# Order of three transfers, of weight splits and of gathers in a kernel of clustered attention and two-level experts

## The chip, the cores and the metric

The kernel runs on one core of one Trainium2 chip. The metric is the device time of one execution in microseconds; a kernel is executed several times and its median is taken. The kernel before takes 748.74 us (median of 3 runs, 743.39 to 748.81).

## The reference

What is computed is an attention over clusters, whose output is the input of a mixture of experts with two levels of routing. Cut to what matters (shapes: batch 4, 8 heads, 768 positions, head size 64, 16 clusters; then 3072 tokens of 512, 4 groups of 4 experts, hidden size 1024):

```python
q_assign = argmax(einsum('bhsd,hcd->bhsc', q_n, c_n), axis=-1)     # normalised q, centroids
k_assign = argmax(einsum('bhsd,hcd->bhsc', k_n, c_n), axis=-1)
mask = q_assign[:, :, :, None] == k_assign[:, :, None, :]
scores = where(mask, scale * matmul(q, k.transpose(0, 1, 3, 2)), -1e9)
scores = scores - max(scores, axis=-1, keepdims=True)
attn = exp(scores) / (sum(exp(scores)) + 1e-9)
x = matmul(attn, v)  ->  rows of [3072, 512]

g_idx = argmax(x @ w_group);  g_w = softmax(x @ w_group)[g_idx]
for g in groups:                      # tokens of group g
    e_idx = argmax(xg @ w_expert[g]); e_w = softmax(...)[e_idx]
    for e in experts of g:            # tokens of expert e
        h = maximum(xg[mask_e] @ w1[g, e], 0.0)
        out[tok_idx] = (g_w * e_w)[:, None] * (h @ w2[g, e])
```

## The kernel before, in words

The work is one stream of matmuls on TensorE with the other engines beside it. Float32 operands are split in two float16 halves (a high part, and what is left of it), and a product is made of three products of halves.

**Attention.** Heads go through in turn (32 of them, numbered over batch and head). A coarse pass (`coarse`) makes scores and their maxima; `rowmax` (from L326) transposes the maxima, ScalarE copies them from PSUM to the tile `mr` (L345), and a transfer on SyncE's queue (SP) puts them into row 80 of the head's operand tile A (L347). The fine pass (`fine`, L355 on) makes the scores with two matmuls (L360 with A, L361 with B), exponentials on ScalarE (L365), the low part on GpSimd or VectorE (L372), and `av` multiplies by V (L392). The head needs its `mr` before the first L360 of its fine pass.

**Routing.** When a batch's heads are done, `Router.decide` finds group and expert of each token, and GpSimd scatters token number and gate into a table in HBM, one slot per token, by expert (L711).

**Expert A.** `Experts.first` takes the expert with the most tokens so far and loads and splits its weights while attention still runs. `fetch` (L889 on) is a generator that the attention's schedule advances a step at a time ("yield"): it waits until the third of the four batches has been routed, waits READ = 5 further steps, reads the expert's slots from the table (`tabA`, three transfers, L893) and the table itself (`tb`, L894) on SP's queue, converts the ids, gathers the rows on GpSimd (L975) into the tiles `qx`, `kx`, `vx`, with 3 steps behind each, and transposes them by three SP transfers into `xTA` (L919). Part A is the feed-forward network of that expert on these rows (matmuls of L1013, up, and L1035, down), with 288 slots.

**Ranks.** `ranks` (L1314) goes through the remaining work: rank -1 takes the last batch's tokens of expert A (128 slots, `xTB`), ranks 0 to 14 take one expert each, sorted by their number of tokens, with 288 slots and fewer. A rank has 8 steps, each one of the up matmuls (12 matmuls into a PSUM tile `psh`, evacuated by ScalarE to `hh` at L1015 and split by VectorE to `hl` at L1016), a piece of the down matmuls of the rank before (L1035 into `psy`, evacuated at L1038 `yh` and L1039 `yl`, or L1049), `settle` (L1075, L1088), the transposition of the next rank's tokens (`tokens`, L985 and L987, at step 5), and the making of weights: `stream` is a generator which loads 512 KB of float32 weights per step (`load_chunk`, L801, on SP's queue into tile `st`, five loads ahead, six tiles) and splits them (`split_chunk`: high part on ScalarE L808 or GpSimd L810, low part on VectorE L811). There are 8 parts a rank, four of w1 and four of w2; FILL says at which steps of a rank the generator is advanced. The tiles of one rank's w1 are wh0a and wl0a, of the next rank's wh0b and wl0b, those of w2 wh1b or wh. A tile of `psh` is free again when `hl` has been made; there are three.

**Order.** Each engine executes its instructions in the order in which the program lists them. The scheduler places instructions by the dependencies and by `issue_after(x)`, which puts what follows behind instruction x in the list of x's engine. SP's and GpSimd's queues of transfers are lists in the same way: a transfer that waits holds what stands behind it.

## Time and profile before

| | us |
|---|---|
| median of 3 runs | 748.74 (743.39 to 748.81) |
| the profiled execution, its time | 746.08 |
| its span (first to last instruction) | 744.3 |
| around the span | 1.8 |
| mean granted clock of TensorE | 0.989 of full speed |

Times in the trace are counted from the start of the span. Busy time is that in which an engine executes an instruction; the rows of a timeline give the start, the duration, the instruction with what it writes and reads and, in brackets, how long its engine had been idle and what ended that. "SPq" is the queue of transfers that SyncE issues. The span has 26030 instructions.

### The profile page before, as it was taken

To read this page: it belongs to the slowest core of one execution; us is meant where nothing else is said; L and a number is where in the kernel's file an instruction comes from. 1 tells how busy PE (TensorE), PEld (TensorE's weight loads), DVE (VectorE), ACT (ScalarE), POOL (GpSimd) and SP (SyncE) were. 2 spreads that over 40 slices of the span, in tenths; PEclk is the share of its full clock that TensorE was granted. 3 is DMA by queue.
4 is the path that set the end of the run, shared out by engine and by line. 5 is a ranking of instruction groups with operands and counts; after the bars stand their busy time and mean duration, and the time that the engine had idled before them with its cause. 6 is when DMAs were issued, how large, how long until landed. Compare 5 with 4: busy or idle time off the path is not lost.

```text
span 744.3 us, 26030 instructions
## 1 busy us (share of the span) xinstructions
PE 712.3 (96%) x10672; PEld 608.8 (82%) x10672; DVE 601.0 (81%) x1246; ACT 473.2 (64%) x913; POOL 498.4 (67%) x526
## 2 busy tenths in 40 slices
PE   5899999999999999999899989999999999999996
PEld 3677888887788888888687866887789999999995
DVE  5999989898998989988977547766778888898861
ACT  4558798897979879777873364444444455555542
POOL 9678897899988999889962354244554545564522
PEclk9999999999999999999999989999999999999999
DMA  8856737457584756517650886877688688888811
GB/s 256 192 163 174 199 90 192 124 152 156 102 207 98 174 137 132 120 21 185 130 106 26 219 303 202 258 220 219 214 259 258 221 275 279 246 281 277 262 62 51
DMA packets 115719, 134.74 MB, mean 181 GB/s; under 512 B 34963, under 2 KB 85651, under 8 KB 115592
## 3 DMA queue, kind: packets, MB, share of 16 engines
q1 hardware_dynamic: 109820, 119.61, 58.7%
q0 software_dynamic: 5616, 13.35, 5.1%
q8 instruction: 85, 1.39, 0.8%
q14 instruction: 42, 0.34, 0.2%
q10 hardware_dynamic: 156, 0.03, 0.0%
HBM read 93.20 MB, written 14.11 MB: 144 GB/s over the span
## 4 chain that ended last, share of the span: by engine, by line
PE 63%; DVE 18%; ACT 6%; issue 5%; DMA 3%; POOL 2%; another core or an unknown queue 1%; POOLq 0%; SPq 0%; ACTq 0%; DVEq 0%
PE psh L1013 15%; PE pso L392 11%; PE psy L1035 10%; PE psf L360 6%; PE psf L361 5%; PE psc L318 5%; DVE mpart L321 5%; PE psy L1049 3%; ACT p L365 2%; DMA st<-w 2%; PE psm L251 2%; DVE wl0a L811 1%; PE psm L985 1%; PE psm L1075 1%
## 5 line engine op out<-in xcount | busy, mean ns | idle before, releaser
L372 POOL TENSOR_TENSOR pl<-p 128x512 f16<-128x512 f32 x212 | 218.2, 1052 | 28.1 <-ACT p L365 25.7
L365 ACT ACTIVATE p<-psf 128x512 f32<-128x512 f32 x288 | 171.4, 598 | 51.4 <-PE psf L361 41.7
L321 DVE TENSOR_REDUCE mpart<-psc 128x1 f32<-128x512 f32 (+1 forms) x282 | 189.0, 682 | 17.6 <-PE psc L318 15.6
L392 PE MATMUL pso<-V,pl 128*128 128x65 f16 x2040 | 165.0, 193 | 0.0
L360 PE MATMUL psf<-A 82*128 82x384 f16 (+2 forms) x576 | 144.2, 275 | 2.5 <-DMA A<-mr 2.0
L361 PE MATMUL psf<-B 128*128 128x384 f16 (+2 forms) x576 | 144.1, 275 | 0.0
L392 PEld LDWEIGHTS <-p 128*128 128x128 bf16 x1776 | 124.4, 98 | 23.3 <-issue 1.2
L392 PEld LDWEIGHTS <-pl 128*128 128x128 f16 x2040 | 134.7, 97 | 1.3 <-issue 0.4
L392 PE MATMUL pso<-V,p 128*128 128x65 f16 x1776 | 132.9, 193 | 0.0
L318 PE MATMUL psc<-A 80*128 80x512 f16 (+1 forms) x376 | 107.0, 328 | 4.5 <-DVE mpart L321 3.2
L1016 DVE SCALAR_TENSOR_TENSOR hl<-psh,hh 128x160 f16<-128x160 f32 (+14 forms) x136 | 50.3, 370 | 66.0 <-ACT hh L1015 50.2
L372 POOL TENSOR_TENSOR pl<-p,ph 128x512 f16<-128x512 f32 x66 | 76.0, 1158 | 21.0 <-POOL pl L372 8.8
L1015 ACT ACTIVATE hh<-psh 128x160 f16<-128x160 f32 (+14 forms) x136 | 46.3, 345 | 66.7 <-PE psh L1013 62.4
L1013 PE MATMUL psh<-xT,wh0a 128*128 128x288 f16 (+7 forms) x512 | 74.7, 255 | 0.0
L1013 PE MATMUL psh<-xT,wh0b 128*128 128x272 f16 (+6 forms) x448 | 65.2, 254 | 1.7 <-DVE xT L987 0.7
L975 POOL DMA_INDIRECT xg<-xbuf,ri x32 | 40.0, 1251 | 38.7 <-PE psm L985 21.8
L361 PEld LDWEIGHTS <-B 128*128 128x128 f16 x576 | 56.8, 99 | 10.7 <-issue 1.9
L360 PEld LDWEIGHTS <-A 82*128 82x128 f16 x576 | 55.7, 98 | 11.5 <-DMA A<-mr 2.0
L1013 PE MATMUL psh<-xT,wl0a 128*128 128x288 f16 (+7 forms) x256 | 64.0, 255 | 0.0
L1089 POOL DMA_INDIRECT out_dram<-y,ri x32 | 38.4, 1200 | 32.3 <-ACT y L1088 25.9
L1013 PE MATMUL psh<-xT,wl0b 128*128 128x272 f16 (+6 forms) x224 | 55.9, 253 | 0.0
L1013 PEld LDWEIGHTS <-wh0a 128*128 128x128 f16 x512 | 46.6, 98 | 4.9
(327 smaller groups left out, 1657.9 us busy)
## 6 DMA issues: line engine op xcount, KB each, us to landing
st<-w SPq DMA_DIRECT2D x128, 512.0 KB
B<-parts SPq DMA_DIRECT2D x64, 192.0 KB
kx<-kT SPq DMA_DIRECT2D x16, 384.0 KB
qx<-qT SPq DMA_DIRECT2D x16, 384.0 KB
vx<-vr SPq DMA_DIRECT2D x16, 384.0 KB
A<-parts SPq DMA_DIRECT2D x32, 192.0 KB
xbuf<-xs SPq DMA_DIRECT2D x16, 384.0 KB
A<-mk SPq DMA_DIRECT2D x56, 24.0 KB
```

The source lines that it names most:

```text
L318: last["mm"] = nc.tensor.matmul(out=pc[:, off:off + k1 - k0], lhsT=QA[h % 8][0:80, c * P:(c + 1) * P], rhs=KA[h % 8][0:80, k0:k1], start=T ...
L321: nc.vector.tensor_reduce(out=(mp[:, 0, 0:1], mp[:, :, 1], mp[:, 1, 0:1])[i], in_=pc.rearrange("p (a x) -> p a x", a=n), axis=AX.X, op=ALU ...
L360: nc.tensor.matmul(out=o, lhsT=KA[h % 8][0:82, ks], rhs=QA[h % 8][0:82, q0:q1], start=True, stop=False)
L361: nc.tensor.matmul(out=o, lhsT=KBs[h][:, ks], rhs=QBs[h][:, q0:q1], start=False, stop=True)
L365: cfg["exp"] = nc.scalar.activation(out=p32, in_=pf, func=AF.Exp, scale=QK / (SQ * SQ))
L372: lo = (nc.vector if u in (EARLY if h < 2 else DVE_LO[h % 8] if h < NH - 2 else DVE_END) else nc.gpsimd).tensor_tensor(out=pl, in0=p32, in ...
L392: nc.tensor.matmul(out=O[:, col:col + v.shape[-1]], lhsT=p[:, bs], rhs=v, start=c == 0 and q == 0 and i == 0, stop=c == NCH - 1 and i == l ...
L975: self.got = nc.gpsimd.indirect_dma_start(out=xg[0:n].rearrange("p k a x -> p (k a x)"), out_offset=None, in_offset=bass.IndirectOffsetOnA ...
L1013: self.mm = nc.tensor.matmul(out=ph[:, 0:M], lhsT=w[:, k, fs], rhs=xT[:, a, k], start=i == 0, stop=i == 3 * KD - 1)
L1015: nc.scalar.activation(out=hh[:, f], in_=ph[:, 0:M], func=AF.Relu)
L1016: self.ev = nc.vector.scalar_tensor_tensor(out=hl[:, f], in0=ph[:, 0:M], scalar=0.0, in1=hh[:, f], op0=ALU.max, op1=ALU.subtract)
L1035: self.mm = nc.tensor.matmul(out=py[:, 0:M], lhsT=w[:, f, d * P:(d + 1) * P], rhs=a[:, f], start=i == 0, stop=i == len(prods) - 1)
```

## The change

Three things are altered. First, `rowmax` keeps its transfer in cfg["mr"], and `fetch` waits two more steps before it reads the table, and lists these reads behind the latest such transfer; the steps behind each gather become two instead of three. Second, FILL: in rank -1 the generator of weights is advanced at steps 0, 2, 4 and 6 alone (four parts instead of eight), in rank 1 twice in each of the first four steps (twelve instead of eight), in all other ranks once in each step as before. Third, the gathers of rank k + 2 are written down at rank k instead of those of rank k + 1.

```diff
@@ -344,7 +344,7 @@
         mr = sm.tile([NCH, P], F16, name="mr")
         nc.scalar.copy(out=mr, in_=tp[0:NCH, 0:P])
         ready.add(("max", h))
-        last["mr"] = (nc.scalar if h == 2 else nc.sync).dma_start(out=QA[h % 8][80:81].rearrange("o (c x) -> o c x", x=P), in_=mr)
+        last["mr"] = cfg["mr"] = (nc.scalar if h == 2 else nc.sync).dma_start(out=QA[h % 8][80:81].rearrange("o (c x) -> o c x", x=P), in_=mr)
 
     def fsegs(u):
 
@@ -743,7 +743,7 @@
     ADD = 5
     SLOTS = 13
     SLT = 12
-    FILL, SETTLE, TOK = (0, 1, 2, 3, 4, 5, 6, 7), 2, 5
+    FILL, SETTLE, TOK = {-1: (1, 0, 1, 0, 1, 0, 1, 0), 1: (2, 2, 2, 2, 1, 1, 1, 1)}, 2, 5
     HI = (0, 1, 0, 1, 0, 1, 0, 1)
     LEAD = 12
 
@@ -886,9 +886,9 @@
         self.tb = self.small("tb", [R.E, self.nt * P, 2])
         while R.done < R.B - 2:
             yield
-        for _ in range(READ):
+        for _ in range(READ + 2):
             yield
-        with self.after():
+        with self.after(), self.tc.issue_after(self.cfg["mr"].ins) if "mr" in self.cfg else ExitStack():
             for t, n in enumerate(sz):
                 R.reads(nc.sync.dma_start(out=tab[0:n, t], in_=tv[t * P:t * P + n]))
             R.reads(nc.sync.dma_start(out=self.tb, in_=R.table.rearrange("(e s) w -> e s w", s=R.BS)[0:R.E, 0:self.nt * P]))
@@ -911,7 +911,7 @@
             if rows:
                 with self.tc.issue_after(self.cfg["lo"].ins) if "lo" in self.cfg else ExitStack():
                     self.gather(ids[0:n, t:t + 1], n, xgs[t], rows)
-            for _ in range(3):
+            for _ in range(2):
                 yield
         xTA = self.wa.tile([P, KD, 2, CA], F16, name="xTA")
         self.xTA = xTA.rearrange("p k a m -> p a k m")
@@ -1314,11 +1314,12 @@
     def ranks(self, bg):
 
         E, sizes = self.R.E, self.sizes
-        xT, xgs, down = self.xTB, self.xg0, iter(())
+        xT, nxt, down = self.xTB, self.xg0, iter(())
         for k in range(-1, E - 1):
             M = self.caps[k] if k >= 0 else P
-            if 0 <= k < E - 2:
-                xgs = self.gathers(k + 1)
+            xgs = nxt
+            if k < E - 3:
+                nxt = self.gathers(k + 2)
             h = []
             up = self.up(xT, M, self.weights_of(k, 0) if k >= 0 else self.WA[0:2], h)
             for i in range(8):
@@ -1328,7 +1329,7 @@
                 next(down, None)
                 if i == (self.SETTLE if k >= 0 else 6):
                     self.settle()
-                if i in self.FILL:
+                for _ in range(self.FILL[k][i] if k in self.FILL else 1):
                     with ExitStack() as order:
                         for op in (self.kept, self.turned, self.got, self.yev[min(1 + i // 2, 3)]) if k < 0 else (self.ev,):
                             order.enter_context(self.tc.issue_after(op.ins))
```

What the edits move in the engines' lists is seen at three places.

SyncE's queue, near the end of attention. `A_171<-mr` and `A_172<-mr` are the row maxima of two heads, `tabA` and `tb` the reads of the table, `xTA` the three transposes that part A reads, `xTr` a transpose for the routing, `xbuf` the store of token rows; ISA rows stand in front of transfers whose address comes from a register. Before:

```order
L893 ISA
L893 DMA tabA<-table 128x2
L347 DMA A_171<-mr 1x6x128
L893 ISA
L893 DMA tabA<-table 128x2
L893 ISA
L893 DMA tabA<-table 32x2
L894 DMA tb<-table 16x768
L347 DMA A_172<-mr 1x6x128
L919 DMA_TRANSPOSE xTA<-qx 128x8x128
L598 DMA xbuf<-xs 128x6x256
L919 DMA_TRANSPOSE xTA<-kx 128x8x128
```

After:

```order
L347 DMA A_171<-mr 1x6x128
L893 ISA
L893 DMA tabA<-table 128x2
L893 ISA
L893 DMA tabA<-table 128x2
L893 ISA
L893 DMA tabA<-table 32x2
L894 DMA tb<-table 16x768
L347 DMA A_172<-mr 1x6x128
L598 DMA xbuf<-xs 128x6x256
L919 DMA_TRANSPOSE xTA<-qx 128x8x128
L613 DMA_TRANSPOSE xTr<-xs 128x12x128
```

The first row maxima now stand in front of the three reads of the table, the second where they stood; the transposes from `qx` and `kx` each stand one place later, behind the store and the transpose of `xTr`; in both lists the one from `vx` is the last of the three.

ScalarE's list, rank -1. `yh` is the evacuation of part A's result, `wh0a`, `wh0b` and `wh1b` are high parts of weights, each of which waits for its own load; the loads in order have the semaphores DMAHW4, 5, 6, 7, 0, 1, 2, 3. Before:

```order
L1205 CAST xT<-psm 128x512 [waits PE_49]
L808 ACTIVATE wh0a<-st 128x2x512 [waits DMAHW4_49]
L808 ACTIVATE wh0a<-st 128x2x512 [waits DMAHW5_49]
L1038 ACTIVATE yh<-psy 128x288 [waits PE_49]
L808 ACTIVATE wh0a<-st 128x2x512 [waits DMAHW6_49]
L808 ACTIVATE wh0a<-st 128x2x512 [waits DMAHW7_49]
L1038 ACTIVATE yh<-psy 128x288 [waits PE_49]
L808 ACTIVATE wh0b<-st 128x2x512 [waits DMAHW0_49]
L1015 ACTIVATE hh<-psh 128x128 [waits DVE_49,PE_49]
L808 ACTIVATE wh0b<-st 128x2x512 [waits DMAHW1_49]
L1015 ACTIVATE hh<-psh 128x128 [waits PE_49] x2
L808 ACTIVATE wh1b<-st 128x4x256 [waits DMAHW2_49]
```

After:

```order
L1205 CAST xT<-psm 128x512 [waits PE_49]
L808 ACTIVATE wh0a<-st 128x2x512 [waits DMAHW4_49]
L808 ACTIVATE wh0b<-st 128x2x512 [waits DMAHW0_49]
L1038 ACTIVATE yh<-psy 128x288 [waits PE_49]
L808 ACTIVATE wh0a<-st 128x2x512 [waits DMAHW5_49]
L808 ACTIVATE wh0b<-st 128x2x512 [waits DMAHW1_49]
L808 ACTIVATE wh1b<-st 128x4x256 [waits DMAHW2_49]
L1038 ACTIVATE yh<-psy 128x288 [waits PE_49]
L1015 ACTIVATE hh<-psh 128x128 [waits DVE_49,PE_49]
L808 ACTIVATE wh0a<-st 128x2x512 [waits DMAHW6_49]
L1015 ACTIVATE hh<-psh 128x128 [waits PE_49]
L808 ACTIVATE wh0a<-st 128x2x512 [waits DMAHW7_49]
```

In front of the first `yh` here stands the split of the fifth load (DMAHW0) in place of the second's; three splits instead of two precede the second `yh`.

VectorE's list, same place. `ri` holds the ids for the gathers of ranks 0 on, `rg` the gates, `yl` the low part of part A's result, `hl` the low part of the hidden values. Before:

```order
L1211 TENSOR_SCALAR bi<-psm 128x1
L1212 TENSOR_SCALAR bg<-psm 128x1
L811 SCALAR_TENSOR_TENSOR wl0a<-st,wh0a 128x2x512 x2
L1103 CAST ri<-psm 128x48
L1104 TENSOR_SCALAR rg<-psm 128x48
L1039 SCALAR_TENSOR_TENSOR yl<-psy,yh 128x288
L811 SCALAR_TENSOR_TENSOR wl0a<-st,wh0a 128x2x512 x2
L1039 SCALAR_TENSOR_TENSOR yl<-psy,yh 128x288
L811 SCALAR_TENSOR_TENSOR wl0b<-st,wh0b 128x2x512
L1016 SCALAR_TENSOR_TENSOR hl<-psh,hh 128x128 x3
```

After:

```order
L1211 TENSOR_SCALAR bi<-psm 128x1
L1212 TENSOR_SCALAR bg<-psm 128x1
L811 SCALAR_TENSOR_TENSOR wl0a<-st,wh0a 128x2x512
L1039 SCALAR_TENSOR_TENSOR yl<-psy,yh 128x288
L1103 CAST ri<-psm 128x48
L1104 TENSOR_SCALAR rg<-psm 128x48
L811 SCALAR_TENSOR_TENSOR wl0a<-st,wh0a 128x2x512
L1039 SCALAR_TENSOR_TENSOR yl<-psy,yh 128x288
L1016 SCALAR_TENSOR_TENSOR hl<-psh,hh 128x128
L811 SCALAR_TENSOR_TENSOR wl0a<-st,wh0a 128x2x512
```

Two of the four low parts of weights in front of the first `hl` go behind it or later, as does the one of `wl0b`; `ri` now stands behind the first `yl`.

GpSimd's list of gathers (L975) is the same before and after in all rows but those near the end of rank 0, where two splits (L810) change sides with gathers. SyncE's list of weight loads (L801) is the same.

## Rows read from the trace of the kernel before

**Rows 1.** Part 1 of the page: busy time of each engine, its share, its instructions.

```profile
PE 712.3 (96%) x10672; PEld 608.8 (82%) x10672; DVE 601.0 (81%) x1246; ACT 473.2 (64%) x913; POOL 498.4 (67%) x526
```

**Rows 2.** Busy time by stretches, with the columns: granted clock, DMA share and GB/s last.

```profile
core 0: us, PE busy (x) PEld busy (x) DVE busy (x) ACT busy (x) POOL busy (x), PEclk, DMA share, GB/s
...
369.40:371.35 1.95, 0.01 (x1) 0.01 (x1) 1.76 (x8) 1.09 (x2) 1.95 (x2) 1.00 0.04 1
371.35:376.50 5.15, 5.15 (x75) 4.28 (x76) 2.91 (x8) 3.73 (x7) 1.06 (x2) 0.67 0.07 13
...
427.00:442.50 15.50, 11.80 (x150) 10.71 (x148) 7.89 (x16) 9.87 (x19) 8.62 (x9) 0.78 0.88 297
```

**Rows 3.** Timeline of TensorE at 371: start, duration, instruction, idle time before it.

```profile
371.35 0.34 PE L360 MATMUL psf<-A 82*128 82x384 f16 x1 [1.95 <-DMA A<-mr]
```

**Rows 4.** Timeline of ScalarE at 363: the row maxima.

```profile
363.30 0.24 ACT L345 COPY mr<-psm 6x128 f16<-6x128 f16 x1
```

**Rows 5.** Waits of SyncE's queue, 340 to 480: total us, times, longest.

```profile
SPq L893 <- DMA table<-pay,rdi: 4.9, 1, 4.9
```

**Rows 6.** Timeline of SyncE's queue, 362 to 398: issues.

```profile
369.14 0.35 SPq L893 DMA_DIRECT2D tabA<-table  x1
369.54 0.74 SPq L347 DMA_DIRECT2D A<-mr  x1
...
386.28 1.71 SPq L613 DMA_TRANSPOSE xTr<-xs  x1
388.12 1.91 SPq L919 DMA_TRANSPOSE xTA<-vx  x1
```

**Rows 7.** Timeline of TensorE, rank -1.

```profile
429.14 0.38 PE L1049 MATMUL psy<-wh,hh 128*128 128x512 f16 x1
...
435.10 0.37 PE L1013 MATMUL psh<-xT,wh 128*128 128x128 f16 x2 [3.17 <-DVE hl L1016]
...
436.33 2.24 PE L985 MATMUL psm<-ident,xg 128*128 128x128 f16 x24
```

**Rows 8.** Timeline of ScalarE, rank -1.

```profile
421.23 0.41 ACT L1038 ACTIVATE yh<-psy 128x288 f16<-128x288 f32 x1 [0.29 <-PE psy L1035]
...
424.49 1.06 ACT L808 ACTIVATE wh0a<-st 128x1024 f16<-128x1024 f32 x1 [1.90 <-DMA st<-w]
...
427.64 1.05 ACT L808 ACTIVATE wh0b<-st 128x1024 f16<-128x1024 f32 x1
...
434.44 0.28 ACT L1015 ACTIVATE hh<-psh 128x128 f16<-128x128 f32 x1 [4.06 <-remote]
```

**Rows 9.** Line 1013 by operands: count, ns min/median/max, first and last start us.

```profile
L1013 PE MATMUL psh<-xTA,wh x64: 282/286/286, 392.8 to 406.4; 128*128 128x288 f16 x64
L1013 PE MATMUL psh<-xT,wh x64: 216/219/314, 427.1 to 442.4; 128*128 128x128 f16 x64
L1013 PE MATMUL psh<-xT,wh0a x64: 286/286/297, 442.5 to 460.0; 128*128 128x288 f16 x64
```

**Rows 10.** One split's instructions on ScalarE and VectorE, ns min/median/max.

```profile
L808 ACT ACTIVATE wh0a<-st x18: 1039/1056/1078, 418.9 to 698.6; 128x1024 f16<-128x1024 f32 x18
...
L811 DVE SCALAR_TENSOR_TENSOR wl0a<-st,wh0a x6: 1209/1218/1226, 420.0 to 458.9; 128x1024 f16<-128x1024 f32 x6
```

**Rows 11.** Busy time by stretches: rank 1, columns as in rows 2.

```profile
461.00:485.00 24.00, 23.48 (x205) 19.32 (x205) 17.04 (x24) 11.25 (x23) 8.13 (x9) 1.00 0.86 271
```

**Rows 12.** Timeline of VectorE, rank -1: the gather ids.

```profile
424.29 0.21 DVE L1103 CAST ri<-psm 128x48 int32<-128x48 f32 x1 [1.90 <-PE psm L1228]
```

**Rows 13.** Timeline of GpSimd, rank -1: the first gather.

```profile
425.37 1.60 POOL L975 DMA_INDIRECT xg<-xbuf,ri  x1 [10.89 <-DMA st<-w]
```

**Rows 14.** Waits of all engines, 405 to 465: a split for its load.

```profile
ACT wh L808 <- DMA st<-w: 4.7, 2, 3.0
```

**Rows 15.** Timeline of SyncE's queue, 405 to 445: the weight loads.

```profile
410.62 29.84 SPq L801 DMA_DIRECT2D st<-w  x14
```

**Rows 16.** Chain that ended last, 637 to 700: a late load.

```profile
669.53 5.09 DMA st<-w
```


## The prediction

> **What bounds the kernel now.** Read first the page's first part: TensorE's matmuls fill 712.3 of 744.3 us, 96%, and the next engine, VectorE, 81% [rows 1]. Shorter work elsewhere can only help where TensorE waits, and all its idle time is 32 us. So the second view is the table of busy time by stretches, laid over the places that the change touches, because it shows two things a share cannot: idle TensorE and its granted clock [rows 2]. Two stretches stand out. From 369.40 to 371.35 TensorE did nothing (0.01 us busy), and in the 5.15 us behind it the clock granted was 0.67. From 427.00 to 442.50 it was busy for 11.80 of 15.50 us at a granted clock of 0.78. A clock of 1.00 is 2.4 GHz, the lower level is 1.2 GHz, half; a mean clock c over a stretch of t therefore loses t x (1 - c) of work. That is 5.15 x 0.33 = 1.70 us behind the first gap, 15.50 x 0.22 = 3.41 us in the second stretch. In both the fall came behind an idle gap. (The second stretch is rank -1: its up matmuls begin at 427.1, those of rank 0 at 442.5 [rows 9].) The first place is worth 1.95 + 1.70 = 3.65 us, the second 3.70 + 3.41 = 7.1 us, together 1.4% of the span. These are the two places that the change can touch; everything else is looked at for harm.
>
> Third, the waits there. At 371.35 the matmul of L360 had waited 1.95 us for the copy of the row maxima into A [rows 3]. ScalarE had made those maxima at 363.30 + 0.24 = 363.54 [rows 4]. In SP's own order the row-maxima copy stands behind the first read of the slot table, and that read waited 4.9 us for the scatters into the table [rows 5]; SP issued it at 369.14 and the copy at 369.54 [rows 6]. So some 6 us old maxima stood in line behind a read that nobody needed yet. In the second stretch TensorE waited 3.17 us (ended 435.10) for a slot of hidden activations that VectorE had not split [rows 7], VectorE waited for ScalarE, and ScalarE's evacuation of psh at 434.44 had waited 4.06 us for something that the trace names only "remote" [rows 8].
>
> **The change part by part. Edit 1, the table read.** It takes two engines' waits apart: the copy is issued first. It needs only ScalarE's copy (done 363.54) and one SP transfer long before, so it goes out near 364 and is there some 2 us later (issue 369.54 to matmul 371.35 was 1.81 [rows 3, 6]), at 366, over 3 us before TensorE wants it at 369.40. Removed: 1.95 of idle and the 1.70 of half clock that follows it. Not all of it comes back: ScalarE was the engine next to full before the gap, and where TensorE runs on, it must evacuate without the pause. In the 1.95 us of the gap ScalarE was busy for 1.09 [rows 2], work which now lies beside TensorE's. I take off some 0.45 us: 3.65 - 0.45 = 3.2. From below 2.2 (all 1.09 and some of its tail is still waited for), from above 3.65. Two more yields delay the read of the table, one yield less per gather takes this back; the third row-maxima copy keeps its place behind the read, and had time before.
>
> What is late next: the copy's place is taken by what follows it. The three transposes into xTA feed the first part A matmul at 392.8 [rows 9]. SP ended issuing the last at 388.12 + 1.91 = 390.03, behind a 1.71 us transpose of xTr [rows 6], so it landed within 2.75 us. If TensorE comes 3.2 us earlier, it is there at 389.6. The scatters that the table read waits for do not come earlier, the vector instructions between which the gathers stand do. So the last transpose ends between 386.8 (all moves along) and 390.03 (nothing does), and the wait is 0 in the first case and, with 2.75 to land, at most 3.2 in the second. I take 0, because its gathers are bound to instructions that move along with TensorE; both ends stay in the range.
>
> **Edit 2, where the splits are made.** A split is one ScalarE (or GpSimd) instruction of 1.06 us and one on VectorE of 1.22 us [rows 10]. Rank -1 is given 4 instead of 8, so VectorE sheds 4 x 1.22 = 4.9 us in front of the hidden-activation splits; rank 1 gets 4 more, 12 in all. Rank 1's stretch of 24 us had VectorE busy 17.04 us, ScalarE 11.25 and GpSimd 8.13 [rows 11]. VectorE comes to 17.04 + 4.9 = 21.9 of 24, 91%; ScalarE to 13.4, GpSimd to 10.2. Twelve loads are 6.3 MB, and at 271 GB/s [rows 11] the stretch moves 6.5. It fits in front of what TensorE does there, so 0; from above, a pair of splits in front of a copy of xT would cost 2 x 1.22 = 2.4, from below 0, since TensorE was idle for just 0.5 us there.
>
> In rank -1 the order on ScalarE is what matters, and it does not simply get shorter. Before, the third yh evacuation (421.23) stood behind two splits of the first two loads. Now the fifth load's split is in front of it, and ScalarE takes its instructions in turn: yh waits until that load has landed. The fourth held ScalarE for 1.90 us until 424.49, and the fifth's split ran at 427.64 [rows 8]. So the fifth landed between about 424.5 and 427.6; I take 426. Split 1.06, yh 0.41, three more splits 3.2, the last yh 0.41, the first hh 0.28 and as much for hl: TensorE gets its first slot back at 426 + 5.6 = 431.6. It has work until 429.14 [rows 7] and so is idle 2.5 us; before it was 3.70 in the whole stretch. Gain 1.2, and 1.0 with the reordered transposes. I do not give back the 3.41 of the clock, since 1.95 us of idle sufficed to lose it at 371. Queued behind yh is also VectorE's conversion of the gather ids: ri, at 424.29 before [rows 12], now comes after the yl that needs this yh, at about 427.8, and the gathers, first at 425.37 [rows 13], 3.4 us later. The transposes that want them ran at 436.33 [rows 7]; three gathers at the first one's 1.60 us are issued by 428.8 + 4.8 = 433.6, so this still fits, with little over. Range of this edit: -3.0 to +3.0, where the upper end is the 3.0 us longest wait of a split for its load near here [rows 14].
>
> When does the fifth load land? Five loads of 512 KB were issued from 410.62 on [rows 15]. The Trainium skill, DMA: Bandwidth & Descriptors, Specifications, gives one core about 358 GB/s from memory; estimate by it: 2.62 MB take 7.3 us, so the fifth would be there at some 418, before yh is due, and edit 2 would bring rival A's time. The trace disagrees so far: the fourth came at 424.49 [rows 8] and the whole stretch behind it moved 297 GB/s [rows 2]; the measurement decides.
>
> **Edit 3, gathers one rank ahead.** GpSimd's queue of gathers stands in the same places as before; they were hoisted as far as their six buffers allow. Near the end of rank 0 two splits change sides with three gathers. 0; from both sides one gather or split, 1.1 us.
>
> **The sum** on the profiled execution: 746.08 (span 744.3 and 1.8 around it) - 3.2 - 1.0 + 0 = 741.9. The median of the runs shown, 748.74, is 2.7 above that execution; the same saving from it gives 744.5. I forecast between the two, 743.
>
> **The rivals.** (A) Faster: the 4.06 us of "remote" disappears with the calmer transfers, or the fifth load is early. Then TensorE has no gap in rank -1 and no half clock: 3.70 + 3.41 = 7.1 instead of 1.0, 746.08 - 3.2 - 7.1 = 735.8, 738.4 from the median. For it: VectorE has 4.9 us less; against it: ScalarE's queue is fuller at the decisive place, and that wait was not for a split. (B) Slower: one mechanism, ScalarE held by a late load in front of yh. Price: later in the run a load was late by 5.09 us [rows 16]. Landing at 427.6 + 5.1 = 432.7, TensorE restarts at 438.3, idle 9.2 instead of 3.7: +5.5 - 3.2 = +2.3, 748.4. It decides from a landing at 430.4 on, where edit 1's gain is gone. For it: four loads stand in front of TensorE's first slot; against: the fourth came at 424.49 with the same queue before it. (C) The transposes into xTA become the wait: 1.6 to 3.2 of edit 1 goes, 743.5 to 745.1.
>
> **How the numbers follow.** Forecast 0.50 (own range 740 to 746), A 0.22, C 0.15, B 0.13. About 1%, 7.5 us, is what a measurement of this kernel can tell from no change. A lies beyond it from either base mostly (0.20), the forecast with its lower end (0.12): 0.32 faster. B's tail and what I have not seen give 0.06 slower; 0.62 within. The range goes from A's middle, 736, to B's, 749.
>
> **What would show it.** Right: no idle TensorE near 369 and the clock 1.00 there; the row-maxima copy at 364 in SP's queue; in rank -1 ScalarE's yh behind a wait for a load, TensorE idle about 2.5 us, clock still under 0.9. Wrong: an idle TensorE in front of the first xTA matmul (C); rank -1 at clock 1.00 (A); over 9 us idle there (B); or TensorE waiting for splits in ranks 1 and 2, which I priced at nothing.

## The result and the profile of the kernel after

The changed kernel took 750.12 us (median of 20 runs, 746.70 to 753.83), the kernel before 746.10 in the same session: ratio 1.0053, interval 1.0037 to 1.0069. It is slower by half a per cent, where I had forecast 743.0 and a gain. By the bound of 1% this is no change; but the interval excludes a gain, and the time lies 1.1 us above my range.

The profiled execution of the kernel after has a span of 747.2 us (744.3 before). Its page, part 1:

```profile
PE 711.9 (95%) x10672; PEld 607.5 (81%) x10672; DVE 607.3 (81%) x1246; ACT 473.2 (63%) x913; POOL 508.4 (68%) x526
```

TensorE has the same work to 0.4 us [rows 1]; the 2.9 us of span are waiting. Where, is seen in the table of busy time by stretches, with the granted clock, DMA share and GB/s last:

```profile
core 0: us, PE busy (x) PEld busy (x) DVE busy (x) ACT busy (x) POOL busy (x), PEclk, DMA share, GB/s
369.40:371.35 1.95, 1.95 (x56) 1.81 (x55) 1.95 (x5) 1.95 (x5) 1.95 (x3) 1.00 0.00 0
371.35:376.50 5.15, 4.62 (x99) 4.01 (x96) 4.00 (x14) 4.96 (x11) 3.30 (x4) 1.00 0.08 13
427.00:440.50 13.50, 10.13 (x144) 8.69 (x142) 6.30 (x14) 9.25 (x18) 10.38 (x10) 0.92 0.69 235
440.50:458.00 17.50, 17.14 (x134) 11.99 (x132) 8.14 (x12) 8.35 (x15) 5.31 (x5) 0.97 0.47 146
458.00:472.00 14.00, 9.86 (x68) 7.09 (x66) 9.95 (x14) 4.70 (x10) 5.83 (x6) 0.88 0.80 255
```

The first place is as I forecast: TensorE is busy for all of the 1.95 us and for 4.62 of the 5.15 behind it, at a clock of 1.00, where it had stood still for 1.95 us and then run at 0.67 [rows 2, 3]. SyncE's queue in the timeline of the kernel after shows the reason; the copy goes out at 365.03, 5.5 us ahead of the reads:

```profile
365.03 0.75 SPq L347 DMA_DIRECT2D A<-mr  x1
370.50 1.45 SPq L893 DMA_DIRECT2D tabA<-table  x3
```

Rank -1 (427.00 to 440.50) still has 3.4 us of idle and a clock of 0.92. Rank 0 behind it is almost full, but the transfers run at 146 GB/s. The stretch from 458.00 on holds the end of rank 0 and, from 460.23, the first half of rank 1, in which TensorE before was busy for 23.48 of 24 us [rows 11]; now it is idle for 4.1 of 14 us at a clock of 0.88. The two ranks in ScalarE's timeline:

```profile
424.54 1.06 ACT L808 ACTIVATE wh0b<-st 128x1024 f16<-128x1024 f32 x1 [5.16 <-DMA st<-w]
425.50 0.39 ACT L1038 ACTIVATE yh<-psy 128x288 f16<-128x288 f32 x1
...
436.58 1.06 ACT L808 ACTIVATE wh0b<-st 128x1024 f16<-128x1024 f32 x1 [1.80 <-DMA st<-w]
437.55 0.74 ACT L987 COPY xT<-psm 128x512 f16<-128x512 f16 x2
...
464.33 1.06 ACT L808 ACTIVATE wh<-st 128x1024 f16<-128x1024 f32 x1 [3.36 <-DMA st<-w]
465.30 0.68 ACT L1015 ACTIVATE hh<-psh 128x288 f16<-128x288 f32 x2
```

Each of the three is a split that waits for its load, with something TensorE needs queued behind it: `yh`, then the copies of `xT`, then `hh`. TensorE's waits at these places (the first two rows are of rank -1, the rest of rank 1):

```profile
429.77 0.27 PE L1013 MATMUL psh<-xT,wh 128*128 128x128 f16 x2 [1.08 <-DVE hl L1016]
...
438.16 0.22 PE L1075 MATMUL psm<-back,yh 128*128 128x128 f16 x1 [2.09 <-issue]
...
460.23 0.28 PE L1013 MATMUL psh<-xT,wh0b 128*128 128x272 f16 x1 [1.20 <-DVE xT L987]
...
461.02 0.28 PE L1013 MATMUL psh<-xT,wh0b 128*128 128x272 f16 x1 [0.52 <-ACT xT L987]
...
465.74 0.40 PE L1035 MATMUL psy<-hh,wh1b 128*128 128x288 f16 x1 [2.43 <-ACT hh L1015]
```

The 2.43 us in front of 465.74 fall into the 3.36 us that ScalarE waited at 464.33. The 2.09 us in front of 438.16, for which the view names no releaser ("issue"), end 0.05 us after the first copy of `xT` behind the split of 436.58 (it runs to 438.11); in the second profile of this kernel, below, the same row of L1075 waits for "ACT xT". The 1.20 and 0.52 us at the start of rank 1 have another reason: VectorE, which made splits from 456.70 and 458.20 on, came to its copies of `xT` at 459.33, and no load was waited for. The chain of what ended last passes through two of the three loads (start, us, what):

```profile
412.66 11.86 DMA st<-w
...
458.03 6.28 DMA st<-w
```

### The profile page after: what moved, and what is told of

Its sections match the earlier page's. It is cut to its first block, busy times and chain, and to the rows that moved or that the text cites. A ratio compares the mean times of both kernels' runs of the same rounds, so it can differ in the third digit from the quotient of the medians.

```text
span 747.2 us, 26024 instructions
## 1 busy us (share of the span) xinstructions
PE 711.9 (95%) x10672; PEld 607.5 (81%) x10672; DVE 607.3 (81%) x1246; ACT 473.2 (63%) x913; POOL 508.4 (68%) x526
## 4 chain that ended last, share of the span: by engine, by line
PE 55%; DVE 15%; DMA 10%; ACT 7%; POOL 6%; issue 5%; SPq 2%; POOLq 0%; DVEq 0%; ACTq 0%
PE psh L1013 14%; PE psy L1035 9%; PE pso L392 9%; DMA st<-w 5%; PE psf L360 5%; PE psf L361 5%; PE psc L318 5%; DVE mpart L321 3%; PE psy L1049 3%; POOL pl L372 3%; ACT p L365 2%; DMA qx<-qT 2%; PE psm L251 2%; PE psm L1075 1%; DVE wl0a L811 1%
## 5 line engine op out<-in xcount | busy, mean ns | idle before, releaser
L975 POOL DMA_INDIRECT xg<-xbuf,ri x32 | 41.6, 1300 | 32.4 <-ACT wh0a L808 13.5
L1089 POOL DMA_INDIRECT out_dram<-y,ri x32 | 41.0, 1283 | 31.6 <-ACT y L1088 26.3
```

Of the source, the lines that this page charges most:

```text
L975: self.got = nc.gpsimd.indirect_dma_start(out=xg[0:n].rearrange("p k a x -> p (k a x)"), out_offset=None, in_offset=bass.IndirectOffsetOnA ...
```

## The experiments

Two questions: which edit does the harm, and by what mechanism. The kernels of this section ran in three sessions; a ratio is to the kernel before in its own session (742.68, 736.94 and 742.17 us), with the 95% interval. To place the differences I use the length of five stages in each profile, between the first starts of matmuls: of the routing on `xTr` (L630), part A (`psh<-xTA`), rank -1 (`psh<-xT,wh`), rank 0 (`wh0a`), rank 1 (`wh0b`) and rank 2 (`wh0a` again). They are worked out by subtracting starts such as those of [rows 9], in us:

| kernel | ratio | to part A | part A | rank -1 | rank 0 | rank 1 |
|---|---|---|---|---|---|---|
| before | 1 | 23.98 | 34.37 | 15.33 | 18.51 | 24.45 |
| after | 1.0053 | 22.25 | 34.39 | 13.81 | 19.91 | 28.60 |
| after, again (e11) | 1.0077 | 22.67 | 33.01 | 12.33 | 19.28 | 25.36 |
| edit 1 (e1) | 0.9975 | 22.67 | 33.02 | 13.92 | 18.56 | 23.77 |
| edit 2 (e2) | 1.0047 | 22.43 | 34.29 | 12.59 | 17.91 | 25.71 |
| edit 3 (e3) | 0.9999 | 22.24 | 33.01 | 10.98 | 17.80 | 23.77 |
| paid in rank 0 (e5) | 0.9985 | 22.68 | 33.01 | 14.00 | 19.00 | 24.29 |
| never paid (e6) | 1.0598 | 22.83 | 34.69 | 13.31 | 18.83 | 26.64 |
| half loads (e9) | 1.0041 | 22.68 | 33.02 | 12.66 | 19.14 | 24.45 |
| half loads, eight splits (e10) | 0.9995 | 22.69 | 34.69 | 9.79 | 17.79 | 23.77 |
| registers bound (e12) | 1.0027 | 22.70 | 33.01 | 13.88 | 18.03 | 25.76 |
| one move, ids behind (e13) | 0.9951 | 21.27 | 33.01 | 14.78 | 18.70 | 23.77 |
| one move (e14) | 0.9960 | 21.23 | 33.02 | 12.86 | 17.79 | 23.77 |
| e13 with registers bound (e15) | 0.9949 | 21.29 | 33.02 | 13.43 | 17.80 | 23.77 |

**Edit 1 alone.** The changes of `rowmax` and `fetch`; FILL and the gathers of ranks as before. The cut is against the kernel after.

```diff
-    FILL, SETTLE, TOK = {-1: (1, 0, 1, 0, 1, 0, 1, 0), 1: (2, 2, 2, 2, 1, 1, 1, 1)}, 2, 5
+    FILL, SETTLE, TOK = (0, 1, 2, 3, 4, 5, 6, 7), 2, 5
```

> Edit 1 alone (row maxima ahead of the table read; weight splits as in the kernel before). Theory T, each edit acts for itself and the loss of the changed kernel lies in edit 2: the 1.95 us gap and its half clock go, about 1.4 us is given back where VectorE waits for the table rows, net about -1.7 us, ratio to before 0.998 (0.996 to 0.9995), and TensorE keeps the lead to the end. Rival S, the stream of weights is the limit of the ranks and takes back whatever TensorE gains: the lead is gone by rank 1 or 2, ratio 1.000, and TensorE waits there for splits as in the changed kernel.

Measured: 0.9975 (0.9947 to 1.0003), most likely a quarter of a per cent faster. The gap is gone, but part comes back twice within 20 us, seen in the timeline of TensorE of this kernel:

```profile
372.59 0.22 PE L342 MATMUL psm<-ident,mh 128*128 128x128 f16 x1 [0.74 <-DVE idA L901]
...
388.20 0.23 PE L392 MATMUL pso<-V,pl 128*128 128x65 f16 x2 [0.29 <-DVE pl L372]
...
389.74 0.24 PE L392 MATMUL pso<-V,pl 128*128 128x65 f16 x2 [0.88 <-POOL pl L372]
```

**Edit 2 alone.** FILL as in the kernel after, all else as before.

> Edit 2 alone (four splits in rank -1, twelve in rank 1; table read as before). Theory T: the 4 to 5 us loss at the end of rank 0 and the start of rank 1 is edit 2's own, less some 1 to 2 us that it gains in rank -1: +4 to +5.7 us, ratio 1.005 to 1.008, with TensorE idle over 2 us and a granted clock under 0.95 around the first matmuls of rank 1. Rival S (whatever arrives early is taken back by the weight stream): TensorE arrives 2 us later than in the changed kernel, so the wait at rank 1 is 2 us shorter and the ratio stays at the changed kernel's 1.005 or below, toward 1.002.

Measured: 1.0047 (1.0019 to 1.0074). The harm is in edit 2, though not as I expected it: the profile has no wait over 2 us at the start of rank 1, but 0.39, 0.52 and 0.64 us there, at a clock of 1.00. The two ratios together give 0.9975 x 1.0047 = 1.0022, with some 0.004 of uncertainty to either side; the kernel after lies near the upper end of this with its first ratio, 1.0053, and above it with a second one, 1.0077.

**Edit 3 alone.** The gathers one rank ahead; FILL and `fetch` as before (the cut is against the kernel before).

```diff
-            if 0 <= k < E - 2:
-                xgs = self.gathers(k + 1)
+            xgs = nxt
+            if k < E - 3:
+                nxt = self.gathers(k + 2)
```

> Edit 3 alone: every engine's list of instructions is the same as in the kernel before, but for line numbers. Every theory: ratio 0.998 to 1.002. Its profile is a second one of the kernel before: if the gap of TensorE at 369 us is there again, edit 1 removes something that every execution has (theory T); if the table read waited much less than 4.9 us for the scatters and there is no gap (rival V), what edit 1 saves differs from execution to execution and the first profile showed a large case.

Measured: 0.9999 (0.9983 to 1.0016). Without edit 2, every engine's list is the one of before except for line numbers, so this is also a second profile of the kernel before. The first place, in TensorE's timeline of edit 3 alone:

```profile
370.14 0.34 PE L360 MATMUL psf<-A 82*128 82x384 f16 x1 [1.20 <-DMA A<-mr]
```

The gap is 1.20 us instead of 1.95, and the clock stayed at 1.00. Rank -1 took 10.98 us instead of 15.33, with the same list. So most of the 7.1 us that I found there in the profile before (3.70 idle, 3.41 of clock), and ScalarE's wait of 4.06 us for "remote" [rows 8], belonged to that execution and not to the order; 1.91 us of idle are left in this one.

**The owed parts paid in rank 0.** The kernel after, with the four additional splits one rank earlier.

```diff
-    FILL, SETTLE, TOK = {-1: (1, 0, 1, 0, 1, 0, 1, 0), 1: (2, 2, 2, 2, 1, 1, 1, 1)}, 2, 5
+    FILL, SETTLE, TOK = {-1: (1, 0, 1, 0, 1, 0, 1, 0), 0: (2, 2, 2, 2, 1, 1, 1, 1)}, 2, 5
```

> The changed kernel, but the four splits left out of rank -1 are made up in rank 0 and not in rank 1. Theory T in detail: in rank 0 of the changed kernel the transfers ran at 146 GB/s since six tiles of loaded weights stood unsplit, and the four parts owed were then all wanted in rank 1. Paid in rank 0, the loss at rank 1 (4.8 us in the trace) shrinks to 0 to 2: ratio to before 0.997 to 1.001. Rival Q, the loss is ScalarE's order (splits in front of the evacuation of psh) wherever many splits are packed: it moves into rank 0 and stays as large, ratio 1.004 to 1.007.

Measured: 0.9985 (0.9960 to 1.0011), against 1.0053 for the kernel after. Rank 1 takes 24.29 us, and rank 0 19.00 with twelve splits, less than the kernel after takes there with eight in its two profiles (19.91 and 19.28). So it is not that splits leave rank -1 which harms, but how long they stay owed.

**Never paid.** Four parts in rank -1, eight in each rank from 0 on.

```diff
-    FILL, SETTLE, TOK = {-1: (1, 0, 1, 0, 1, 0, 1, 0), 1: (2, 2, 2, 2, 1, 1, 1, 1)}, 2, 5
+    FILL, SETTLE, TOK = {-1: (1, 0, 1, 0, 1, 0, 1, 0)}, 2, 5
```

> The changed kernel, but the four splits left out of rank -1 are not made up at all: every rank from 0 on makes eight, and the stream runs four parts later to the end. Theory T (twelve parts in one rank are more than the transfers and VectorE give): no loss at rank 1, ratio 0.996 to 1.000, with a wait at the very end of at most 2 us. Rival L, the loss is the lost lead itself, not the twelve: with four parts less in hand TensorE waits in rank 1 as in the changed kernel, and in later ranks again, ratio 1.005 or more.

Measured: 1.0598 (1.0550 to 1.0647); rival L, by far more than its 1.005. The waits of ScalarE's splits for loads in the whole span of this kernel (total us, times, longest):

```profile
ACT wh0a L808 <- DMA st<-w: 43.9, 15, 5.6
ACT wh0b L808 <- DMA st<-w: 42.0, 13, 6.7
...
ACT wh L808 <- DMA st<-w: 34.4, 13, 5.0
ACT wh1b L808 <- DMA st<-w: 32.2, 14, 4.8
```

These are 152.5 us in 55 waits; the kernel before has 18.3 us in 14. The four parts are the stream's lead: a load needs a staging tile, and that comes free by a split. As long as they are owed, each split meets its load as it lands. It is the same wait as in ranks 0 and 1 of the kernel after, made permanent.

**The kernel after again**, beside edit 3 alone and the two that follow.

> The changed kernel once more, beside the others on one chip. Theory T: ratio 1.003 to 1.007, and a second profile shows again a gap of TensorE over 1.5 us at the start of rank 1 behind a split that waits for its load. Rival N, the gap at rank 1 in the first profile was an accident of that execution and the loss is spread otherwise: no gap over 1 us there, with the ratio as before.

Measured: 1.0077 (1.0052 to 1.0102). The wait of 2.43 us for `hh` in rank 1 did not come back at that size: TensorE waits 0.40 and 0.52 us for `xT` there and 0.57 us for `hh`. By my own sign that is rival N: the large gap was of one execution, and the loss is spread. The loads issued from 405 to 484 us, the row of L801 on SyncE's queue (count; ns min/median/max; first and last start): the kernel after again, then edit 3 alone, the list of before.

```profile
L801 SPq DMA_DIRECT2D st<-w x29: 372/373/399, 406.5 to 483.4; - x29
```

```profile
L801 SPq DMA_DIRECT2D st<-w x32: 372/373/408, 407.0 to 482.4; - x32
```

At the first matmul of rank 1 (454.69 and 452.37 us) 16 and 20 of them are out: the four that are owed are missing. At that of rank 2 it is 28 and 29, so three are made up in rank 1. Every profile with eight splits in rank -1 has 20 at the start of rank 1, and so has the kernel that pays in rank 0; all others with four have 16. What SyncE's queue waits for there, from 405 to 460 (total us, times, longest), in the kernel after again, in its first profile, and in edit 3 alone:

```profile
SPq L801 <- DVE wl0b L811: 15.1, 4, 10.7
```

```profile
SPq L801 <- DVE hl L1016: 14.9, 2, 13.6
```

```profile
SPq L801 <- DVE wl1b L811: 8.6, 3, 3.6
SPq L801 <- DVE hl L1016: 7.1, 3, 3.8
```

`wl0b` ends a split and so frees a staging tile. For 10.7 us, at the end of rank -1 and in rank 0, no load went out because all tiles held parts that were still owed; the longest in the two rows of edit 3 alone is 3.8. In the first profile the wait is 13.6 us, to 447.24, and it is behind the 146 GB/s of rank 0 (the view names `hl`, but the split of `wl0b` ends there at 447.22). The chain of the kernel after again shows what may be a second cause:

```profile
424.05 0.37 SPq L801
...
424.47 0.28 SPq L837
...
428.42 0.05 SPq L801
...
428.63 3.65 DMA st<-w
...
432.30 1.06 ACT wh0b L808
433.36 0.48 ACT xT L987
```

From 424.47 to 428.42 SyncE reads registers with the numbers of later experts (L837, seven of them, not eight as I wrote above, 0.56 us from one to the next) between two weight loads. Busy time by stretches, first of the kernel after again, then of edit 3 alone:

```profile
422.00:424.90 2.90, 2.90 (x44) 2.68 (x42) 1.77 (x4) 2.90 (x5) 1.59 (x1) 1.00 0.03 10
...
428.40:430.20 1.80, 1.80 (x37) 1.67 (x35) 1.63 (x5) 0.72 (x4) 1.50 (x2) 1.00 0.44 75
...
434.00:438.00 4.00, 4.00 (x30) 2.77 (x29) 0.58 (x2) 3.00 (x6) 3.09 (x4) 0.59 0.76 220
438.00:442.00 4.00, 4.00 (x28) 2.58 (x26) 2.81 (x4) 0.82 (x2) 1.61 (x2) 0.98 0.43 144
```

```profile
422.00:424.90 2.90, 2.90 (x39) 2.58 (x37) 2.16 (x3) 1.10 (x2) 2.39 (x2) 1.00 1.06 360
...
428.40:430.20 1.80, 0.88 (x16) 0.70 (x13) 1.80 (x5) 1.53 (x5) 1.42 (x2) 1.00 0.99 313
...
438.00:442.00 4.00, 4.00 (x27) 2.44 (x25) 2.83 (x4) 0.82 (x2) 0.00 (x0) 1.00 0.84 305
```

Three holes in the transfers, at 10, 75 and 144 GB/s, stand against 360, 313 and 305. The first lies in front of the load of 424.05 and the last in the wait of 10.7 us: no free tile. The middle one is behind the register reads, when that load and the gathers had landed and the next load was just going out.

In SyncE's list, seven register reads in a row stand behind the stream's eighth load; before, six in a row behind the fourteenth. The load after them landed at 432.28, its split held the copies of `xT`, and TensorE waited:

```profile
433.88 0.22 PE L1075 MATMUL psm<-back,yh 128*128 128x128 f16 x1 [1.89 <-ACT xT L987]
```

The 0.59 in the stretch from 434 on is what the clock lost behind this gap: 4.00 x 0.41 = 1.6 us. But neither the wait nor the lowered clock comes from the reads for certain. The same matmul waits behind a split and its load in kernels with eight splits in rank -1 too, 2.06 us in edit 1 alone, 2.90 and 1.45 us in e13 and e14 below, where the six reads in a row come later in the queue. And behind the same wait in edit 2 alone, 2.00 us, the clock stayed at 1.00.

**Half loads.** Two kernels, both with edits 1 and 3, with and without edit 2, in which parts 10 to 23 of the stream load half their rows and the split reads this half twice, so that the transfers halve and the engines' work stays (half of these weights is left out).

```diff
-        nc.sync.dma_start(out=st, in_=we[:, rows, cols])
-        return st
+        m = (rows.stop - rows.start) // (2 if half else 1)
+        nc.sync.dma_start(out=st[:, 0:m], in_=we[:, rows.start:rows.start + m, cols])
+        return (st, m) if half else st
```

> The changed kernel with the loads of parts 10 to 23 of the weight stream halved (256 KB in place of 512; the splits read the loaded half twice, so that every engine's work and order stay; half of the weights of these parts is left out, and the output of the ranks that use them is another). Theory T (the loss at rank 1 is loads that come too late, with ScalarE's evacuations queued behind the splits that wait for them): the 4.8 us loss goes, no wait of a split for its load over 1.5 us in rank 1, ratio to before 0.997 to 1.000. Rival Q (VectorE and ScalarE have too many splits in rank 1, whatever the loads do): ratio stays at 1.003 to 1.007.

> Control for the halved loads: the same halving of parts 10 to 23, in the kernel with edits 1 and 3 and eight splits in every rank, rank -1 too (the same half of the weights is left out). Theory T: nothing waits for these loads on the path, so it equals edit 1 alone, ratio 0.996 to 0.999. Rival Q: the same. If halving speeds up any kernel of this kind, this one falls below 0.995, and the run with twelve splits has to be read against it.

Measured: 1.0041 (1.0027 to 1.0055) with edit 2, 0.9995 (0.9979 to 1.0012) without it. So edit 2 costs some 0.46% with half the bytes, in the range of rival Q. With all of them the kernel after again stands 0.8% above the two kernels of that session without edit 2 (0.9995 and 0.9999), and edit 2 alone cost 0.47%: between nearly half of the loss and none of it needs the bytes, and the runs do not tell which. The stages say more. The pair differs by only 0.7 us in rank 1, but by 2.9 us in rank -1 and 1.4 us in rank 0, where TensorE's wait in front of L1080 (L1075 of the kernel after) is 2.05 us and the clock falls behind it; in part A it is the other way round by 1.7 us, which is none of edit 2's. In rank 1 with half loads TensorE's waits for splits in front of `hh` are gone, and those for `xT` remain:

```profile
454.44 0.28 PE L1018 MATMUL psh<-xT,wh0b 128*128 128x272 f16 x1 [0.53 <-DVE xT L992]
...
455.23 0.28 PE L1018 MATMUL psh<-xT,wh0b 128*128 128x272 f16 x1 [0.52 <-ACT xT L992]
```

The test does not separate cleanly: three high parts still waited 2.4 to 3.8 us for half a load, so what is left of the loss is not proved to be the engines' work alone.

**Register reads bound.** The kernel after, each expert's register read placed behind the weight load that precedes it.

```diff
-        nc.sync.dma_start(out=st, in_=we[:, rows, cols])
+        self.fed = nc.sync.dma_start(out=st, in_=we[:, rows, cols])
...
-                    er[r] = self.load_reg(self.ei[0:1, r:r + 1], self.R.E - 1)
+                    with self.tc.issue_after(self.fed.ins) if r else ExitStack():
+                        er[r] = self.load_reg(self.ei[0:1, r:r + 1], self.R.E - 1)
```

> The changed kernel with SyncE's loads of the expert numbers into registers (L837) bound behind the weight load that precedes them in the program; ScalarE's, VectorE's and GpSimd's lists stay as they are. In the changed kernel eight of them stand between two weight loads of rank -1 and take 4.0 us (424.43 to 428.42 in its second profile), the load behind them lands 3.65 us later, ScalarE's split of it stands in front of the copies into xT, and TensorE waits 1.89 us and then has half the clock. Theory R: without them that load goes out 4 us earlier, this wait and the clock behind it go, 2 to 4 us: ratio to before 1.001 to 1.005 and rank -1 at clock 1.00. Rival O, ScalarE's order alone (split of the ninth load in front of xT) is late because VectorE frees the tile late: the wait stays over 1 us, ratio 1.005 to 1.009.

Measured: 1.0027 (1.0005 to 1.0048), below the second run of the kernel after without overlap and below the first with a little. The wait in front of L1075 (here L1076) is gone, as theory R has it. The clock in the profile of this kernel is 1.00 over the place where it was 0.59:

```profile
434.00:438.00 4.00, 3.79 (x61) 3.45 (x62) 0.52 (x2) 3.73 (x8) 3.09 (x4) 1.00 0.84 293
```

That the bind did this is not shown, since the clock was 1.00 in edit 2 alone as well. Rank -1 is no shorter (13.88 us): TensorE waits 2.21 us there for a slot and 2.02 us for a gather. Rank 0 is down to 18.03 us, rank 1 still 25.76, and the loads issued at the start of rank 1 are still 16. The reads account for part of the loss at most; the missing lead is there without them.

**One move alone.** Of edit 1 only the change of place of `A<-mr`, nothing of edits 2 and 3: the steps added in front of the read are taken from those behind it, and the gathers keep their three (the cut is against edit 1 alone).

```diff
-        for _ in range(READ):
+        for _ in range(READ - 2):
...
-            for _ in range(2):
+            for _ in range(3):
```

> Edit 1's one move alone: on every engine the list of the kernel before, but that the row-maxima copy stands in front of the first table read on SyncE's queue (one place). Theory T1: 1.35 us won at 371, 0.9 given back at 373 by VectorE's conversion of the ids, nothing near 388: 0.4 to 0.6 us ahead at the first matmul of part A, ratio 0.998 to 1.000. Rival: the loss near 388 comes without the gathers' move too, and TensorE is level or behind there.

Measured: 0.9960 (0.9943 to 0.9977). The stage to part A is 21.23 us, against 22.67 with edit 1 as written, and the waits for `pl` near 389 are gone. They came with the gathers' places.

**The ids behind `mh`.** The same, and the conversions of the ids (L901, L902) placed behind `mh` (L326) on VectorE, to take away the wait of 0.74 us at L342.

```diff
-        with self.after():
+        with self.after(), self.tc.issue_after(self.cfg["mh"].ins):
```

> Edit 1's table read without its changes of the gathers, and VectorE's conversions of the ids bound behind the row maxima of the next head (L326), so that they do not hold VectorE while the table is still on its way. Theory T1 (edit 1 wins 1.35 us at 371 and gives it back at two places, 0.9 us where the conversion of the ids holds VectorE and so the transpose of L342, 1.5 us near 388 through the later gathers): both give-backs go, TensorE is 1.3 to 2 us ahead of the kernel before at the first matmul of part A; ratio 0.997 to 0.999. Rival: the time was never edit 1's to win, since part A waits for xTA or for the last heads' evacuations: the lead is under 0.5 us there, ratio 0.999 to 1.001.

Measured: 0.9951 (0.9927 to 0.9976), no different from the move alone. The wait stayed, 0.82 us. TensorE's row and VectorE's timeline:

```profile
371.89 0.22 PE L342 MATMUL psm<-ident,mh 128*128 128x128 f16 x1 [0.82 <-DVE idA L901]
```

```profile
369.66 1.51 DVE L372 TENSOR_TENSOR pl<-p 128x512 f16<-128x512 f32 x1
371.09 0.15 DVE L326 TENSOR_SCALAR mh<-psc 128x6 f16<-128x6 f32 x1
371.16 0.68 DVE L829 TENSOR_TENSOR wl<-psm,wh 128x512 f16<-128x512 f32 x1
371.76 0.14 DVE L901 CAST idA<-tabA 128x1 int32<-128x1 f32 x1
```

`mh` is ahead of the ids here and ends at 371.24, 0.65 us before the matmul that reads it. What ends just before the matmul, at 371.84, is L829, the low part of a weight, which reads a PSUM tile `psm`; L342 writes one. In the move alone L829 ends at 372.19 and the matmul starts at 372.25, in edit 1 alone it is 372.54 and 372.59. So the wait is most likely for the PSUM tile that L829 frees, and the view's "idA" is only what VectorE did next; no run moves L829 to show it. My claim that the place of the conversions was the cause fell.

**Both binds, no edit 2.** The kernel of the last test with the register reads bound.

> The run before last with the register loads bound as in the first one; eight splits in every rank. Theories T1 and R: at least as fast as the ids run, ratio 0.994 to 0.998, and the fastest of all. Rival: in the order of the kernel before the register loads are spread and hold nothing: no difference to the ids run (within 0.1%).

Measured: 0.9949 (0.9932 to 0.9966). Without edit 2 the register reads add nothing that shows. This kernel and the move alone beat both the kernel before and the changed one; between them nothing is told apart.

## Why the prediction was wrong

**Edit 1: mechanism right, size wrong.** I took 3.2 us. As written it is worth 0.25% or 1.9 us, with a lower end at 0; the move alone 0.40%, 3.0 us (1.7 to 4.2). Two steps failed. The first is the removal of "1.95 of idle and the 1.70 of half clock", read from one execution: in a second profile of the same list the gap was 1.20 with no loss of clock, and in edit 2 alone, with the read and the copy in the old order, TensorE had no gap there at all. The stage to part A was 23.98, 22.24 and 22.43 us in these three; with the move alone it is 21.23, so 1.0 to 2.7 us. The second is the give-back. I took 0.45 us and named ScalarE; it was VectorE, 0.74 to 0.85 us at L342, behind its L829 (in the first profile of the kernel after 0.53 us, and there ScalarE had its share, 0.79 us at 380.57). And "one yield less per gather takes this back" was priced at nothing, but costs 1.4 us (22.67 less 21.23), at TensorE's waits for `pl`. The wait in front of `xTA` (rival C) did not decide.

**Edit 2, rank -1: what moves was right, what it yields was not.** I took the fifth load at 426 and `yh` behind it; they came at 424.5 and 425.50. TensorE's idle time in front of a slot was 1.27 us, where I had 2.5; but 2.09 us came on top at L1075, behind the split of 436.58, a second late load that my account did not have. And the comparison, 3.70 us of idle before, was one execution's. Over the profiles of the table with all loads whole, six with eight splits in rank -1 average 13.55 us there (10.98 to 15.33), six with four splits 13.32 (12.33 to 14.00). No gain shows. Rival B did not come about either: it began at a landing of 430.4, and that the time came near B's price is a coincidence. Nor did the early load of rival A, by the estimate from the Trainium skill, DMA: Bandwidth & Descriptors, Specifications (about 358 GB/s, the fifth load at some 418): the chain has it 11.86 us after 412.66, at 424.5.

**Edit 2, rank 1: the step that failed.** "It fits in front of what TensorE does there, so 0." I had added busy times and bytes over 24 us and found room for both. Over the six profiles with eight splits and the four with twelve in rank 1 and whole loads, rank 0 goes from 18.19 to 18.78 and rank 1 from 23.88 to 26.36 us: +0.6 and +2.5, against -0.4 in rank -1 (13.15 us in these four), in sum +2.7 us or 0.36%, beside a measured 0.47% for edit 2. At the start of rank 1 TensorE waited 0.8 to 1.7 us for `xT` and 0.6 to 2.4 us for `hh` in these four; of the six, five have no wait there and one has 1.1 us. With half loads those for `hh` go and those for `xT` stay: the first stand behind one split of `wh` on ScalarE, which waited 3.36, 1.50, 1.57 and 2.09 us for its load in the four; the second are VectorE's splits in front of its copies. The 28.60 us of the first profile hold 1.7 us of lowered clock (0.94) besides, which the other three do not have. The upper end of 2.4 that I gave for a pair of splits in front of `xT` has the right size, but the price was more than that pair: a share does not show that the twelve loads come when their splits come due. I had asked what is late next for edit 1, and not for the stream of loads.

**Not priced at all:** the register reads on SyncE. I compared the weight loads in its list and found them the same; the reads between them had moved up, 4.0 us of queue. What they cost is open.

**Edit 3 at nothing** was right: 0.9999.

**The sum** of 741.9 for the profiled execution was 7.0 below its successor's 748.9. By the stages of the two profiles: to part A -1.7 us where I had -3.2, rank -1 -1.5 where I had -1.0, rank 0 +1.4 and rank 1 +4.2 where I had nothing; +2.3 in place of -4.2, 6.5 of the 7.0. Of rival A the full clock in rank -1 came in kernels of either order (1.00 in edit 2 alone and e12, and in edit 3 alone and e14), so it was no property of the change; the missing gap did not come, since TensorE was idle for 2.5 to 4.6 us there in every profile with four splits.

## What to carry to other kernels

A stretch of idle time and lowered clock in one profile is worth what a second profile of the same list still shows; before pricing its removal, ask for that second one. Work that is put off from a full place must be followed through whatever it frees, here staging tiles and with them the loads' lead: pay the debt back in the very next stage or do not put the work off, since left unpaid it cost 6%; and do not judge the room for it by busy shares. When two things in a queue change places, move only those two, and compare every kind of row in the queue's list, those that move no data too.

## What the runs showed of the hardware

With identical lists, rank -1 took 15.33 and 10.98 us. Part A took about 33.0 us in nine profiles and 34.3 to 34.7 in five, whatever the edits: in two of the five (before, after) TensorE was idle for 1.3 us there in place of 0.3, in the three others (edit 2 alone, never paid, half loads with eight splits) the clock was 0.95. What sets these off is open. A register read costs SyncE's queue 0.56 us, and seven of them in a row are 4.0 us, longer than the 3.65 us in which the load behind them came.

The clock did not follow from the length of a gap. Over the 4 us behind gaps of 1.89, 2.06 and 2.90 us (the kernel after again, edit 1 alone, e13) it was 0.59, 0.61 and 0.64, near the level of 1.2 GHz; behind gaps of 2.00 us (edit 2 alone) and of 2.21 and 2.02 us (e12) it was 1.00, and behind gaps of 0.7 to 1.2 us near 370 too. And it fell without any gap: in edit 2 alone TensorE was busy throughout from 416 to 427 us, and from 423 to 426 the clock was 0.50, the level of 1.2 GHz; over the same matmuls in edit 3 alone it stayed at 1.00. So the half clock that I priced as following from a gap can come without one and stay away behind one.
